# A MoE tail behind attention: two zero fills moved behind the last gather, a gate row broadcast through DRAM, and the last gate digits on POOL

## Chip, cores and metric

One core of a Trainium2 chip. The metric is device time in microseconds, the median of several executions. Engines are named as the profile names them: PE (TensorE), DVE (VectorE), ACT (ScalarE), POOL (GpSimd), SP (SyncE, which here only issues DMAs).

## The reference

Attention over 4 batches, 8 heads, 768 positions and head dimension 64, followed by a mixture of experts over the 3072 rows that come out.

```python
# attention: each query keeps 6 of 24 key chunks of 32, by an upper bound on its scores
ub = sum(max(q * k_min, q * k_max))            # one bound for each query and chunk
top_chunks = argsort(where(causal, ub, -1e9))[..., -6:]
attn = softmax(where(sel & causal, q @ k.T / 8, -1e9))
x = (attn @ v) laid out as (3072, 512)
# mixture of experts: 8 experts of 512 -> 1024 -> 512, top 1, capacity 80
expert_idx = argmax(x @ w_gate); gate_w = softmax(x @ w_gate)[expert_idx]
out = zeros((3072, 512))
for e in range(8):
    tok = rows of expert e; if more than 80: the 80 with the largest gate_w
    out[tok] = gate_w[tok] * (relu(x[tok] @ w1[e]) @ w2[e])
```

At most 640 of the 3072 output rows are computed; all others are zero. So the kernel writes zeros over the whole output (four fills of 1.5 MB, one for each batch of 768 rows) and then scatters the computed rows over them.

## The kernel before

**Order of the work.** Everything is written out by hand in one stream of `op(engine, ...)` calls. A helper, `Sync`, puts in the semaphore waits from the names that each operation reads (`r`) and writes (`w`). Each engine runs its own operations in the order in which they are written. DMAs are issued by SP (`"sp"`), by POOL (`"gpd"`), and at the start by ACT.

**The pair loop.** Sixteen pairs of heads (`i` from 0 to 15, four pairs for each batch) go through a software pipeline. For pair `i` PE computes the scores in six steps, of which ACT takes the exponentials (`scores`, L509, L524, L531); POOL masks the diagonal and adds up the denominators (`folds`, L545 and L554); PE multiplies by the values (`values`, L568), and ACT copies the product (L576). The bounds of the next pair (`bounds`, L472, and `bounds_out`, L479 to L491), the denominators and gate logits of the pair before (`sums`, L581 and L595, then L586 to L651 on DVE), and its rows (`rows`, L641 on PE, `scale_rows`, L661 on DVE and a DMA of SP to `x_rows` in DRAM) are woven in between. `take_q` (L439), `take_r` (L443) and `take_k` (L449 to L456) turn the loaded q and k for the pair after the next. SP loads q and k four pairs ahead and v two pairs ahead.

**Ranking by gate weight.** When a batch is complete, its tokens are ranked within each expert during the next batch's pairs. `kk` is the pair's place in its batch, `bb` the batch being ranked:

- `kk == 0`: the gate weights come out as `gt6`, one column for each of six tiles of 128 tokens (`gate`, L679 to L684). Then all 768 are needed as a row on every partition, `G[:, S:2S]`: `rank_row` does it with six PE transposes of a broadcast column (L716) and a copy by ACT (L718). `rank_own` (L726) is DVE's.
- `kk == 1`: `rank_pred` (L721, ACT) makes a second row, a hair smaller; `rank_cmp` (L741, DVE, six of them) and `rank_diag` (L734) compare each token with all others.
- `kk == 2`: `rank_count` (L791, PE) counts the winners for each expert; `rank_late` makes one-hot rows, digits of the gate weight in three bf16 parts (`gate_digits`, L687 to L690) and columns (`gate_cols`, L694, `gate_gcols`, L699).
- `kk == 3`: `table` and `merge` keep the best 80 of each expert.

**Loads and fills.** Expert weights are loaded with a cast to bf16 by POOL's DMA queue: `wload(e, 0)` is w1 of expert `e`, `wload(e, 1)` its w2, 1 MB each as written. The buffer of w1 of expert 6 holds zeros first, from which three fills are sent (after pairs 0, 1 and 12); the fourth fill comes from a part of `G`, zeroed by ACT at pair 14 (L955). The buffers of w1 of expert 7 and w2 of expert 6 hold the comparisons of `rank_cmp` and `rank_diag`. w2 of expert 7 comes in eight pieces (`last_w2`, L922), four at pair 15 and four among the experts.

**The tail.** The last batch has no later pairs to hide in. Its gate, `last_row` (L708 to L711), comparisons (`last_diag`, `last_low`, `last_high`, L753 to L768, on DVE and ACT), count (`last_count`, L775), table and merge follow the last pair, with `keep_warm` (L886), matmuls into an unused bank, between them. Then `gather` (L1091) fetches 80 rows for each of eight experts by indirect DMA of POOL, `turn` (L1100, L1104) transposes them, `up` (L1114, with ReLU at L1123 on ACT and L1125 on DVE) and `down` (L1138) are the two products. `down` runs in six rounds; DVE scales each round into one of four buffers `yv(r % 4)` (L1142), and POOL scatters it (L1144). Each scatter names all four fills in what it reads, so it waits until all zeros have landed. Gather `e` from 3 on waits for the copy of expert `e - 3`'s `turn`.

Of the kernel before, what the change touches and what calls it, by code (L numbers as in the profile page):

```python
# [147 lines left out]
def bass_quest_chunk_select__then__topk_capacity_drop_kernel(  # L148
# [57 lines left out]
    with ExitStack() as pers:  # L206
# [13 lines left out]

        sy = Sync(nc)
        op = sy.op

        with nc.Block() as blk:

            @blk.sync
            def _body(_unused):
# [41 lines left out]
                gt6 = al(pers, "gt6", [128, NT])  # L269
# [120 lines left out]
                op("dve", lambda: ve.memset(wg[:], 0.0), w=["wg"])  # L390
                op("dve", lambda: ve.memset(onc[:], 0.0), w=["onc"])
# [286 lines left out]
                def gate(b):  # L678
# [4 lines left out]
                    op("dve", lambda: ve.reciprocal(gt6[:], lsum[:]), r=["lsum"], w=["gt6"])  # L683
                    op("dve", lambda: ve.tensor_tensor(ohb[:, :, 0:E], oh[:], along(lmax), ALU.is_equal), r=["oh", "lmax"], w=["ohb"])  # L684

                def gate_digits(b):
                    op("dve", lambda: ve.tensor_copy(gsp[:, :, 0], gt6[:]), r=["gt6"], w=["gsp0"])  # L687
                    op("dve", lambda: ve.tensor_tensor(gdf[:], gt6[:], gsp[:, :, 0], ALU.subtract), r=["gt6", "gsp0"], w=["gdf"])
                    op("dve", lambda: ve.tensor_copy(gsp[:, :, 1], gdf[:]), r=["gdf"], w=["gsp1"])
                    op("dve", lambda: ve.tensor_tensor(gsp[:, :, 2], gdf[:], gsp[:, :, 1], ALU.subtract), r=["gdf", "gsp1"], w=["gsp2"])  # L690

                def gate_cols(b):
                    ohv = [bass.AP(ohb, 0, [[NT * 32, 128], [32, NT], [0, n], [1, E]]) for n in (2, 3)]
                    op("dve", lambda: ve.tensor_tensor(RC[:, :, 0:2, :], ohv[0], bass.AP(  # L694
                        idc, b * NT * 2, [[TOKT * 2, 128], [2, NT], [1, 2], [0, E]]), ALU.mult), r=["ohb", "idc0", "idc1"], w=["RCi"])

                def gate_gcols(b):
                    ohv = [bass.AP(ohb, 0, [[NT * 32, 128], [32, NT], [0, n], [1, E]]) for n in (2, 3)]
                    op("dve", lambda: ve.tensor_tensor(RC[:, :, 2:5, :], ohv[1], bass.AP(  # L699
                        gsp, 0, [[NT * 3, 128], [3, NT], [1, 3], [0, E]]), ALU.mult), r=["ohb", "gsp0", "gsp1", "gsp2"], w=["RCg"])  # L700
# [3 lines left out]
                def last_row():  # L704
                    for t in range(NT):
                        o = t * 128 if t < 3 else 128 + t * 128
                        gb = bass.AP(gt6, t, [[NT, 128], [0, 128]])
# [5 lines left out]
                def rank_row(b):  # L713
                    for t in range(NT):
                        gb = bass.AP(gt6, t, [[NT, 128], [0, 128]])
                        op("pe", lambda: pe.transpose(SC[1][:, ts(t)], gb, ident_f[:]),  # L716
                           r=["gt6", "ident_f"], w=["SC1"], inc=(t == NT - 1))
                    op("act", lambda: ac.activation(G[:, S:2 * S], SC[1][:, 0:S], ACTF.Copy), r=["SC1"], w=["grow"])  # L718
# [4 lines left out]
                def rank_own(b):  # L723
                    tq = bass.AP(triQ, 0, [[128, 128], [0, NT], [1, 128]])
                    gb = bass.AP(gt6, 0, [[NT, 128], [1, NT], [0, 128]])
# [189 lines left out]
                def fill(g, zs, zk):  # L915
                    zd = bass.AP(out.tensor, out.offset + g * NT * 128 * Dm, [[Dm, 128], [128 * Dm, NT], [1, Dm]])
                    op("sp", lambda: sp.dma_start(zd, zs), r=[zk], w=[f"outz{g}"], dsem=f"d_zero{g}")
# [12 lines left out]
                for i in range(NP):  # L930
# [10 lines left out]
                    if i == NP - 1:  # L941
                        wload(E - 1, 0)
# [5 lines left out]
                    if live and kk == 1:  # L948
                        rank_pred()
                        rank_cmp(bb, 5)  # L950
# [3 lines left out]
                    if i == NP - 2:  # L954
                        op("act", lambda: ac.activation(G[:, 0:Dm], bass.AP(ident_f, 0, [[128, 128], [0, Dm]]), ACTF.Copy, scale=0.0),  # L955
                           r=["ident_f"], w=["growP"])
# [9 lines left out]
                    if i:  # L966
# [3 lines left out]
                        scale_rows(i - 1)  # L970
                    if i == NP - 2:
# [176 lines left out]
                for e in range(3):  # L1148
                    gather(e)
# [59 lines left out]
```

## Time and profile before

| what | value |
|---|---|
| median of 3 runs | 290.12 us (290.0 to 290.32) |
| profiled execution: own time, span | 289.86 us, 288.1 us |
| instructions | 8696 |
| busy: PE, DVE, ACT, POOL | 274.3, 213.1, 147.0, 227.2 us |
| pair loop ends, last gather of x issued, last scatter issued | about 236, 270.85, 283.67 us |
| DMA in all | 47.95 MB, mean 166 GB/s |
| the transposes of L716 (18) and the copies of L718 (3) | 273 ns each, 811 ns each |

Times are counted from the start of the span. A timeline line has start, duration, engine, line, operation, tiles written and read, and the count of instructions merged into it; brackets give the idle time just before and what ended it. A line of a DMA issue list has the tiles, the queue, the count, the size, and the time from issue to landing. A line of windows has the stretch, its length, the busy time of PE, PEld (weight loads), DVE, ACT and POOL with their instructions, the granted clock, the share of the 16 DMA engines, and GB/s.

### The profile page before, as it was taken

What the parts mean: (1) busy time and instruction counts of PE and PEld (TensorE: products, weight loads), DVE (VectorE), ACT (ScalarE), POOL (GpSimd) and SP (SyncE); (2) the same over time, 40 slices, a digit from 0 to 9 for tenths busy, and PEclk for the clock granted to TensorE, in tenths of its full rate; (3) what the DMA queues carried; (4) which work ended last, traced back from release to release, by engine and by line L of the source; (5) the groups of instructions that cost most, each with busy time, mean ns of one, the idle gap of its engine ahead of it and who ended that gap; (6) DMA issues with size and microseconds to landing.
All of it is one profiled execution on the core that took longest, in us unless ns stands there. A gap on an engine that the chain in (4) does not pass through costs nothing.

```text
span 288.1 us, 8696 instructions
## 1 busy us (share of the span) xinstructions
PE 274.3 (95%) x3609; PEld 170.0 (59%) x3609; DVE 213.1 (74%) x575; ACT 147.0 (51%) x202; POOL 227.2 (79%) x295
## 2 busy tenths in 40 slices
PE   7899999999999999999999999999999999859991
PEld 7454656565656565656565656666656666428761
DVE  5897455566988989659889898898899888813341
ACT  2275656555576555555765555546756563403310
POOL 6079899998999999989999999899999970044732
PEclk9999999999999999999999999999999999998998
DMA  9999989999989999999999989995991599911361
GB/s 151 180 156 152 320 155 297 169 155 177 187 166 167 193 174 182 158 183 181 164 163 183 186 155 155 183 196 111 298 195 30 220 161 186 208 35 48 89 128 61
DMA packets 158359, 47.95 MB, mean 166 GB/s; under 512 B 142405, under 2 KB 150721, under 8 KB 158320
## 3 DMA queue, kind: packets, MB, share of 16 engines
q1 hardware_dynamic: 141664, 28.34, 50.9%
q0 software_dynamic: 13520, 18.67, 38.4%
q10 hardware_dynamic: 3136, 0.39, 0.9%
q8 instruction: 28, 0.46, 0.7%
q14 instruction: 11, 0.09, 0.1%
HBM read 53.49 MB, written 11.01 MB: 224 GB/s over the span
## 4 chain that ended last, share of the span: by engine, by line
PE 70%; POOL 15%; DVE 6%; DMA 4%; issue 2%; ACTq 1%; POOLq 0%; DVEq 0%
PE SC L509 22%; PE OB L568 19%; POOL ES L554 12%; PE SC L524 4%; PE M L595 4%; PE OB L1138 4%; PE SC L1114 4%; PE OB L641 3%; POOL EXB L545 3%; PE M L472 3%; DMA x_rows<-xp 2%; PE M L581 2%; PE MB L497 2%; DMA qn<-in_q_dram 1%; DMA qn<-x_rows,idx 1%
## 5 line engine op out<-in xcount | busy, mean ns | idle before, releaser
L531 ACT ACTIVATE EXB<-SC 128x1024 f32<-128x1024 f32 x96 | 86.2, 917 | 46.4 <-PE SC L524 45.1
L554 POOL TENSOR_TENSOR ES<-ES,EXB 128x256 f32<-128x256 f32 (+1 forms) x105 | 101.7, 980 | 4.8
L509 PE MATMUL SC<-qT,kT 64*128 64x512 f32 (+3 forms) x512 | 96.3, 466 | 0.1
L568 PE MATMUL OB<-EXB,vn 128*64 128x256 f32 (+3 forms) x704 | 72.8, 361 | 0.7 <-POOL EXB L545 0.7
L568 PEld LDWEIGHTS OB<-EXB,vn 128*64 128x64 f32 x704 | 46.9, 137 | 23.9 <-issue 9.8
L509 PEld LDWEIGHTS SC<-qT,kT 64*128 64x128 f32 x512 | 41.4, 186 | 23.0 <-issue 14.3
L554 POOL TENSOR_TENSOR ES<-EXB 128x768 f32<-128x768 f32 (+1 forms) x30 | 46.8, 1559 | 2.5
L524 PE MATMUL SC<-unsT,ind 64*128 64x128 bf16 (+5 forms) x256 | 37.7, 289 | 0.1
L576 ACT ACTIVATE oT<-OB 128x512 f32<-128x512 f32 (+1 forms) x32 | 15.6, 489 | 38.2 <-PE OB L568 38.2
L545 POOL TENSOR_SCALAR_AFFINE_SELECT EXB<-EXB 128x256 f32<-128x256 f32 x79 | 34.1, 442 | 0.0
L524 PEld LDWEIGHTS SC<-unsT,ind 64*128 64x128 bf16 x256 | 12.8, 95 | 17.9 <-issue 8.0
L439 DVE STREAM_TRANSPOSE qT<-qn 128x768 f32<-128x768 f32 x16 | 15.6, 974 | 7.2 <-PE SC L524 6.4
L586 DVE STREAM_TRANSPOSE M<-M 128x192 f32<-128x192 f32 x16 | 6.3, 394 | 19.2 <-PE M L595 18.9
L1091 POOL DMA_INDIRECT qn<-x_rows,idx x4 | 3.9, 987 | 20.8 <-DMA x_rows<-xp 19.0
L661 DVE TENSOR_TENSOR xp<-OB,rden 128x768 bf16<-128x768 f32 x16 | 15.3, 954 | 6.6 <-PE OB L641 6.3
L443 ACT ACTIVATE rq<-qT 128x768 f32<-128x768 f32 x16 | 13.5, 843 | 9.9 <-DVE qT L439 9.2
L449 DVE STREAM_TRANSPOSE kT<-kn 128x768 f32<-128x768 f32 x16 | 15.5, 966 | 1.2 <-DMA kn<-in_k_dram 1.2
L453 DVE TENSOR_REDUCE kmm<-kT 128x24 f32<-128x768 f32 x16 | 15.2, 950 | 0.5
L454 DVE TENSOR_REDUCE kmx<-kT 128x24 f32<-128x768 f32 x16 | 15.1, 942 | 0.0
L486 DVE MAX8 top<-M 128x8 f32<-128x8 f32 (+4 forms) x160 | 14.6, 164 | 0.6
L641 PE MATMUL OB<-ident_f,oT 128*128 128x128 f32 x96 | 13.9, 281 | 0.5 <-ACT oT L576 0.5
L456 POOL TENSOR_TENSOR kmm<-kmx,kmm 128x24 f32<-128x24 f32 x15 | 7.1, 471 | 9.2 <-DVE wg L907 9.2
(222 smaller groups left out, 415.6 us busy)
## 6 DMA issues: line engine op xcount, KB each, us to landing
w1s<-in_moe_w_dram POOLq DMA_DIRECT2D x8, 1024.0 KB, 9.8
w2s<-in_moe_w_dram POOLq DMA_DIRECT2D x7, 1024.0 KB, 11.2
vn<-in_v_dram SPq DMA_DIRECT2D x32, 192.0 KB, 4.8
kn<-in_k_dram SPq DMA_DIRECT2D x62, 96.0 KB, 2.7
qn<-in_q_dram SPq DMA_DIRECT2D x62, 96.0 KB, 3.1
out_dram<-w1s SPq DMA_DIRECT2D x3, 1536.0 KB, 7.8
x_rows<-xp SPq DMA_DIRECT2D x16, 192.0 KB, 6.1
out_dram<-G SPq DMA_DIRECT2D x1, 1536.0 KB, 6.9
```

The lines of the kernel that those rows point to most:

```text
L439: op("dve", lambda: ve.transpose(qT[j][:], qn[s][:].rearrange("p a b c -> p (a b c)")), r=[f"qn{s}{g}" for g in range(4)], w=[f"qT{j}"])
L449: op("dve", lambda: ve.transpose(kT[j][:], kn[s][:].rearrange("p a b c -> p (a b c)")), r=[f"kn{s}{g}" for g in range(4)], w=[f"kT{j}"])
L453: op("dve", lambda: ve.tensor_reduce(kmm[j][:, 0, 0:NCH], kv, AX, ALU.min), r=[f"kT{j}"], w=[f"kmm{j}"])
L509: op("pe", lambda: pe.matmul(o, kT[j][pr, ts(kt)], qT[j][pr, q0:q1], start=True, stop=False), r=[f"kT{j}", f"qT{j}"], w=[f"SC{s}"], inc=False)
L524: op("pe", lambda: pe.matmul(o, ind[pr, ts(kt)], unsT[j][pr, b0 - 128:q1 - 128], start=False, stop=True), r=[f"ind{h}", f"unsT{j}"], w=[f" ...
L531: op("act", lambda: ac.activation(Ex(st, None, 0, W), src, ACTF.Exp, scale=SCALE), r=[f"SC{s}"], w=[f"E{st}"])
L545: op("gp", lambda: gp.affine_select(ad, a, pattern=[[0, 2], [1, 128]], compare_op=ALU.is_ge, fill=0.0, base=0, channel_multiplier=-1), r=[ ...
L554: op("gp", lambda: gp.tensor_tensor(o, in0, in1, ALU.add), r=[f"E{s2}", f"E{first[0]}"] if first else [f"E{s2}"] + kt, w=kt)
L568: op("pe", lambda: pe.matmul(OB[pr, q0:q1], vn[s][:, kt, h, :], ex, start=(n == 0), stop=last), r=[f"vn{s}{h}", "ES0" if st is None else f ...
L576: op("act", lambda: ac.activation(oT[:, q0:q1], OB[:, q0:q1], ACTF.Copy), r=[f"O{bk}"], w=[f"oT{bk}"])
L641: op("pe", lambda: pe.transpose(OB[:, ts(t)], oT[:, ts(t)], ident_f[:]), r=["oT0", "oT1", "ident_f"], w=[f"O{t // 4}"], inc=(t in (3, NT - ...
L661: op("dve", lambda: ve.tensor_tensor(xo, xi, rx, ALU.mult), r=["O0", "O1", "rden"], w=[f"xp{i % 2}"])
```

## The change

Four things change together.

1. *Gate row, batches 0 to 2.* `rank_row` goes. `gt6` gets 32 columns (zeroed at the start). `row_out` transposes it on DVE in blocks of 32 and sends it to DRAM in token order; `row_in` reads 768 values back to all 128 partitions. Both DMAs are issued by SP. `rank_pred` and the first `rank_cmp` move to later places in `kk == 1`.
2. *Fills.* The fills of batches 2 and 3 leave pairs 12 and 14. ACT zeroes a part of `ES` behind the first three gathers, and SP issues both fills after the last gather has landed. The scatters of rounds 0 and 1 are issued by POOL after that point.
3. *Loads.* w1 of expert 6 is loaded at pair 13 in place of 14, w1 of expert 7 at the end of pair 14 in place of pair 15.
4. *Tail of the last batch.* The digits and columns go to POOL; `gate_gcols` comes earlier; the first product of `values` for the last block comes after `last_row`; `last_low(3)` comes first of ACT's; and the count takes tile 4 last, with four warming matmuls ahead of it in place of six behind.

```diff
+        gd = nc.dram_tensor("gate_row", [32 * 128], F32, kind="Internal").ap()
-                gt6 = al(pers, "gt6", [128, NT])
+                gt6 = al(pers, "gt6", [128, 32])
+                gtT = al(pers, "gtT", [128, 32])
+                op("dve", lambda: ve.memset(gt6[:], 0.0), w=["gt6"])
...
+                def on(b):
+                    return ("gp", gp) if b == B - 1 else ("dve", ve)
+
                 def gate_digits(b):
-                    op("dve", lambda: ve.tensor_copy(gsp[:, :, 0], gt6[:]), r=["gt6"], w=["gsp0"])
+                    e, q = on(b)
+                    op(e, lambda: q.tensor_copy(gsp[:, :, 0], gt6[:, 0:NT]), r=["gt6"], w=["gsp0"])
...
-                def rank_row(b):
-                    for t in range(NT):
-                        gb = bass.AP(gt6, t, [[NT, 128], [0, 128]])
-                        op("pe", lambda: pe.transpose(SC[1][:, ts(t)], gb, ident_f[:]),
-                           r=["gt6", "ident_f"], w=["SC1"], inc=(t == NT - 1))
-                    op("act", lambda: ac.activation(G[:, S:2 * S], SC[1][:, 0:S], ACTF.Copy), r=["SC1"], w=["grow"])
+                def row_out():
+                    op("dve", lambda: ve.transpose(gtT[:], gt6[:]), r=["gt6"], w=["gtT"])
+                    o = bass.AP(gd.tensor, gd.offset, [[32, 4], [128, 32], [1, 32]])
+                    op("sp", lambda: sp.dma_start(o, gtT[:]), r=["gtT"], w=["gd"], dsem="d_gd")
+
+                def row_in():
+                    a = bass.AP(gd.tensor, gd.offset, [[0, 128], [1, S]])
+                    op("sp", lambda: sp.dma_start(G[:, S:2 * S], a), r=["gd"], w=["grow"], dsem="d_gr")
...
-                    if i == NP - 1:
-                        wload(E - 1, 0)
                     folds(i, 0, 1)
...
-                    if live and kk == 1:
-                        rank_pred()
-                        rank_cmp(bb, 5)
                     scores(i, 2, 4)
...
-                    if i == NP - 2:
-                        op("act", lambda: ac.activation(G[:, 0:Dm], bass.AP(ident_f, 0, [[128, 128], [0, Dm]]), ACTF.Copy, scale=0.0),
-                           r=["ident_f"], w=["growP"])
...
                         scale_rows(i - 1)
+                    if live and kk == 1:
+                        rank_cmp(bb, 5)
                     if i == NP - 2:
-                        fill(3, bass.AP(G, 0, [[2 * S, 128], [0, NT], [1, Dm]]), "growP")
                         rank_late(bb)
                     if live and kk == 0:
                         gate_exp()
                         gate(bb)
+                        row_out()
...
+                    if live and kk == 0:
+                        row_in()
                     if i + 4 < NP:
                         load(i + 4, "qk")
...
                     if live and kk == 1:
+                        rank_pred()
                         rank_diag(bb)
...
-                    if live and kk == 0:
-                        rank_row(bb)
-                    if 0 < i < NP - 3:
+                    if 0 < i < NP - 2:
                         wload((i - 1) // 2, (i - 1) % 2)
                     if i == NP - 2:
-                        wload(E - 2, 0)
                         wload(E - 2, 1)
-                    if i in (0, 1, 12):
+                        wload(E - 1, 0)
+                    if i in (0, 1):
...
-                values(NP - 1, (1,), (0, 1), False)
                 gate(b)
                 gate_cols(b)
+                gate_digits(b)
                 sort_take()
-                gate_digits(b)
+                gate_gcols(b)
                 last_row()
-                values(NP - 1, (1,), (1, 9), False)
+                values(NP - 1, (1,), (0, 9), False)
                 last_high(0)
+                last_low(3, "act")
                 last_low(5, "act")
                 values_out(1)
                 last_low(4, "act")
-                last_low(3, "act")
...
                 scale_rows(NP - 1)
-                gate_gcols(b)
-                last_count((0, 5, 1, 4, 2, 3), (0, 0, 0, 0, 0, 6))
+                last_count((0, 5, 1, 3, 2, 4), (0, 0, 0, 0, 4, 0))
...
+                    if r > 1:
+                        scatter(r)
+
+                def scatter(r):
                     op("gpd", lambda: gp.indirect_dma_start(
...
                 for e in range(3):
                     gather(e)
+                op("act", lambda: ac.activation(bass.AP(ES, 0, [[2 * S, 128], [1, Dm]]), bass.AP(ident_f, 0, [[128, 128], [0, Dm]]), ACTF.Copy, scale=0.0),
+                   r=["ident_f"], w=["zero", "D0", "U0", "D1", "L1", "U1"])
...
                             if e + 4 == E - 1:
+                                for g in (2, 3):
+                                    fill(g, bass.AP(ES, 0, [[2 * S, 128], [0, NT], [1, Dm]]), "zero", xgk(E - 1))
                                 last_w2(range(4, FB))
+                                for r in range(2):
+                                    scatter(r)
```

## The prediction

> **What bounds the kernel now.** I read the page's engine line first, then the chain of waits, and then the timelines of POOL, DVE, SP and PE around the places that the change touches.
>
> ```profile
> PE 274.3 (95%) x3609; PEld 170.0 (59%) x3609; DVE 213.1 (74%) x575; ACT 147.0 (51%) x202; POOL 227.2 (79%) x295
> ```
>
> TensorE is busy nearly throughout, but that is no proof that it alone sets the pace. POOL's timeline at the turn of pairs 4 and 5:
>
> ```profile
> 84.03 0.95 POOL L456 TENSOR_TENSOR kmm<-kmx,kmm 128x24 f32<-128x24 f32 x1
> 84.93 0.91 POOL L420 DMA_DIRECT2D w2s<-in_moe_w_dram  x1
> 86.26 0.40 POOL L545 TENSOR_SCALAR_AFFINE_SELECT ES<-EXB 128x256 f32<-128x256 f32 x1 [0.43 <-PE M L595]
> ```
>
> The bracket is all the slack that POOL has in this pair; until 100.6 it has no other gap. An ordinary pair takes 13.9 us on PE, with 0.4 to 0.6 us idle on POOL. DVE in pair 5, where the gate row is used:
>
> ```profile
> 87.23 2.04 DVE L741 TENSOR_SCALAR w2s<-G,gt 128x640 bf16<-128x640 f32 x1
> 89.29 0.96 DVE L661 TENSOR_TENSOR xp<-OB,rden 128x768 bf16<-128x768 f32 x1
> ...
> 90.90 0.98 DVE L439 STREAM_TRANSPOSE qT<-qn 128x768 f32<-128x768 f32 x1 [0.65 <-PE SC L524]
> ```
>
> From 90.90 DVE has no gap until the comparisons end at 102.1, and PE starts the count (L791) at 102.55. So over this batch it is PE's scores, then DVE's 11.2 us, then PE's count that set the pace. The first comparison costs nothing today: the rows for L661 come from PE at 89.26.
>
> The tail is different. The chain of waits has:
>
> ```profile
> 248.64 5.52 DMA x_rows<-xp
> 254.22 0.61 issue
> 255.05 2.75 DMA qn<-x_rows,idx
> 258.17 0.83 PE SC L886 x2
> ```
>
> The last attention rows take 5.52 us to land; the gathers wait on them. The windows show a DMA share over 1 from 233 to 252: three expert loads of 1 MB and four pieces of 128 KB run then. Writing the same rows at 220.9, with the DMA engines idle, took 2.9 us. PE stands still from 254.7 to 257.85 and then runs at half clock:
>
> ```profile
> 259.00:260.00 1.00, 1.00 (x19) 1.00 (x17) 0.00 (x0) 0.00 (x0) 0.57 (x1) 0.50 0.32 82
> ```
>
> (The last three columns are granted clock, DMA share and GB/s.) At the end, POOL scatters each round as soon as DVE has written it:
>
> ```profile
> 269.53 1.02 POOL L1144 DMA_INDIRECT out_dram<-EXB,idR  x1 [0.92 <-ACT kT L1123]
> 270.85 0.98 POOL L1091 DMA_INDIRECT kn<-x_rows,idx  x1 [0.30 <-issue]
> ...
> 283.67 0.97 POOL L1144 DMA_INDIRECT out_dram<-EXB,idR  x1 [2.16 <-DVE EXB L1142]
> ```
>
> **What the Trainium skill says.** "SBUF — State Buffer", section "SBUF: two separate sides": the port pair shared by DVE and GpSimd is an exclusive lock held for the whole instruction, and the loser blocks. The trace agrees: the 2.04 us of L741 above end 0.35 us after a POOL addition (87.11 to 88.92) has ended, while its five sisters take 0.55 to 0.91. "DMA: Bandwidth & Descriptors", section "Issuing engines are not separate DMA queues": all queues run on the same 16 engines and interleave; the 5.52 us against 2.9 agree. "TensorE: Matmul & The Clock Gate", section "What's actually happening": an idle window of about 3.4 us halves the clock; here 3.1 us of idleness were followed by about 3.4 us at 0.5.
>
> **Gate row, three batches.** Removed for each: six transposes, 0.66 us of PE (82.08 in the chain), and ACT's copy, 0.81 us. ACT has gaps in these pairs, so the copy itself gives nothing; I found PE later by 0.66 over L568 to L595, no more. Added: a 32-column DVE transpose, about 0.17 us by the reciprocal's 0.19; DVE idles 1.27 us before the next L586, but L726 ends that much later, and POOL's L456 (0.95 instead of 0.24 beside it) with it. So POOL's 0.43 gap leaves about 0.25 of the 0.66. In pair 12 POOL has no marked gap: about 0. The memset of gt6 lies in DVE's wait for the first load (before 4.65).
>
> Then DVE: the first comparison moves behind L661. With PE 0.66 earlier L661 ends at 89.6; the comparison meets a POOL addition (89.4 to 90.6) and ends near 91.0, against a take_q start of 90.90 before. DVE's chain, and so the count on PE, is then no earlier. rank_pred moves into ACT's gap after L443 (1.2 us) and costs nothing unless that gap goes; then oT is later.
>
> SP: row_out and row_in are two issues of some 0.55 us, and SP stands between them until the row has landed, about 3 us by x_rows' 2.9 to 3.2. Behind it stand the q and k loads for four pairs on; they are used two pairs later (28 us), so this is covered. At batch 0 SP reaches row_out only at 82.0 (x_rows ends its issue there), so row_in goes out near 85.1, beside the expert load of 84.93, and 393 KB land near 89.5 by an estimate of 4.5 us (v pieces of 192 KB took 3.2 to 5.4). DVE wants them at 89.6. Batches 1 and 2 have 4 us or more in hand. **Body: 0**, bounds −1.3 (three times POOL's 0.43) and +2 (DVE waiting for the row).
>
> **Loads and tail.** w1 of expert 6 goes out in pair 13, 14 us earlier, and one of the three issues leaves the end of pair 14 and pair 15 (0.8 us on POOL, beside PE's longer work). One MB at some 200 GB/s is 5.2 us less DMA work before 252, so the last x_rows finds idle engines: issued near 248.4, landed near 251.3. That isn't all gained. The four digit operations (0.7 us) and two column products (0.5 us) leave DVE; on POOL, idle from 236 to 255, they cost some 2 us (six at L456's 0.24 and as much again between them is 2.9 at most) and are done by 245.5, needed at 250. But the count now has 4 warming matmuls of 0.21 us ahead of its last group, and PE gets there later since ACT has one more pair of operations (1.1 us) before oT. My walk along PE gives a count finished at 249.65, against DVE's L796 at 248.75: idx at 252.5 instead of 251.5. The gather goes out 0.8 later, 253.3 instead of 255.05: **−1.75**. PE then waits 0.5 us, not 3.1, so the half-clock stretch (up to 1.2 us; the third gather's landing limits it) gives **−0.85**. The experts run 2.6 us earlier.
>
> **Fills and scatters.** Two fills leave the middle of the kernel, where nothing on the chain waited for them: 0. They return behind gather 7. That gather needs turn(4), whose copy ends at 268.63, now 266.0; with 0.8 to wake and 2.6 to land, 269.4. One fill alone:
>
> ```profile
> out_dram<-G SPq DMA_DIRECT2D x1, 1536.0 KB, 6.9
> ```
>
> and one microsecond of the windows while it ran:
>
> ```profile
> 226.00:227.00 1.00, 1.00 (x17) 0.61 (x12) 0.52 (x3) 0.04 (x1) 1.00 (x3) 1.00 1.04 381
> ```
>
> About 1.2 us pass before it moves data, and then the engines are full at 380 GB/s. So two are not hidden in each other: 3.15 MB / 380 GB/s = 8.3 us, after 270.6. The four pieces of w2 (issued by POOL from 267.8) take about 2 us of this (0.5 MB at 200 GB/s, part of it before 270.6), and 0.2 for the end: **both zeroes landed at 281.1**. Every scatter waits for all zeroes. POOL stands with scatter 0 from about 270, and the other five are queued behind it. Round 4's product writes the buffer of round 0, so DVE waits for scatter 0 to land, the ReLU of expert 7 is queued behind it, and PE's last product behind that. From 281.1: 0.85 for POOL to start (as 254.2 to 255.05), 2.9 to land, 0.75 and 0.5 on DVE, 48 matmuls 1.35 at full or 2.7 at half clock after this long wait, taken as 2.0, 0.6 for the last copy, 0.8 to the scatter: last scatter at 289.5 against 283.67. The serial scatters on POOL, six at 1.3 us, come out 0.4 earlier, so DVE's way decides. With the 4.4 us from there to the end (283.67 to 288.1) the span is 294.0, **+5.9 us**: own time 289.86 + 5.9 = 295.8. The median shown lies 0.26 above the profiled execution's own time: **296.0**.
>
> **Rivals.** (a) *Faster:* the fills land before they hold anything. From the landing to the last scatter I have 8.4 us, so the point is a landing at 275.3, 5.8 before mine. If two fills took the 6.9 us of one, with w2 beside them, it would be 276.3; with the body at −2.0 (PE's transposes in full) and idx not delayed (−0.9) 273.4, so an end at 286.2 and 288.2 us as median. For it: PE's 95%, and the fact that packets of different queues interleave. Against it: the share of 1.04 while one fill ran alone. (b) *The row comes late:* each us by which row_in misses 89.6 stops DVE and with it the count; 1 us in each batch on top gives 299. For it: SP's loads in this stretch took up to 9.6 us. Against it: batches 1 and 2 are early. (c) *A smaller loss:* w2 costs the fills nothing, the clock stays up and the body gives 1.3: 292.5. The transposes' 0.66 us not arriving at all is part of the forecast, not a rival.
>
> **Numbers.** Forecast with (c) 0.75, (b) 0.10, (a) 0.12, and 0.03 for an end within 0.2% (0.6 us, about what a measurement of this kernel can tell from no change). The range runs from 291.5 (below (c)) to 299.0.
>
> **What would show it.** Right: x_rows' last landing near 3 us; PE without half clock at 258; L741's first comparison behind L661 and L791 no earlier in its batch; out_dram from ES landing some 11 us after gather 7; POOL idle about 10 us before scatter 0; DVE idle before the fifth L1142; PE idle some 8 us ahead of the last product. Wrong: the fills landed before round 3 is written, or pairs 5, 9 and 13 shorter by 0.5 us or more, or longer by 1.

## The result, and the profile after

| | before | after |
|---|---|---|
| median of runs | 290.06 us (289.51 to 290.32) | 299.69 us (297.57 to 303.46) |
| profiled execution: own time, span | 289.86, 288.1 us | 298.05, 296.3 us |
| pair loop ends (denominators of the last pair, PE) | 236.65 | 235.92 |
| gather 0, gather 7 issued | 255.05, 270.85 | 252.76, 266.05 |
| last scatter issued | 283.67 | 291.81 |

The ratio is 1.031, interval 1.0221 to 1.04: slower, as forecast, and by more than forecast. Ratios here leave out runs more than 1.5% above the fastest of the same kernel, in after the one of 303.46 us, whose mean granted clock (0.971) is no lower than that of the others (0.966 to 0.975). The other three are 297.57, 298.05 and 301.33; the median of all four is 299.69, that of the three 298.05. That the three lie almost 4 us apart, where before stays within 0.8, is part of what has to be explained.

In after, lines moved a little: the comparisons are L753, `scale_rows` L665, `row_out` and `row_in` L726 and L730, gathers L1097, ReLU of DVE L1131, `down` and its scaling L1144 and L1148, scatters L1154, fills L929. The page's engine line:

```profile
PE 272.6 (92%) x3589; PEld 168.0 (57%) x3589; DVE 210.1 (71%) x573; ACT 144.8 (49%) x199; POOL 228.4 (77%) x301
```

PE has 1.7 us less to do and the kernel is 8 us longer: nothing here is decided by busy time. **The pair loop**, the timelines of POOL and DVE where they were shown of before:

```profile
85.12 0.91 POOL L424 DMA_DIRECT2D w2s<-in_moe_w_dram  x1
86.05 0.41 POOL L549 TENSOR_SCALAR_AFFINE_SELECT ES<-EXB 128x256 f32<-128x256 f32 x1
```

```profile
88.81 0.96 DVE L665 TENSOR_TENSOR xp<-OB,rden 128x768 bf16<-128x768 f32 x1 [1.90 <-PE OB L645]
89.69 1.07 DVE L753 TENSOR_SCALAR w2s<-G,gt 128x640 bf16<-128x640 f32 x1
90.68 0.96 DVE L443 STREAM_TRANSPOSE qT<-qn 128x768 f32<-128x768 f32 x1
```

POOL's bracket is gone: it was the 0.43 us of slack. POOL now sets the pace of the pair, and over the whole chain of waits its additions make 22% of the span where they made 12%. The first comparison stands behind L665, and DVE's next step starts 0.22 us earlier than before (90.68 against 90.90). SP in the same pair:

```profile
70.87 8.16 SPq L368 DMA_DIRECT2D kn<-in_k_dram  x4
...
81.40 0.65 SPq L726 DMA_DIRECT2D gate_row<-gtT  x1
84.21 0.35 SPq L730 DMA_DIRECT2D G<-gate_row  x1
```

The transposed gate column was ready at 78.1, but SP was issuing four loads of k for 8.2 us, then v and `x_rows`, and sent it at 81.40; then SP stood until it had landed and asked for it back at 84.21. The row landed 3.7 us later, 1.8 us ahead of DVE. In the next two batches the margins were 2.8 us (issued 140.60, 3.4 to land, wanted at 146.76) and 2.0 us (198.76, 3.9, 204.71). In this execution the row is in time; it is close.

**The tail.** The windows, with the columns as before:

```profile
259.00:260.00 1.00, 1.00 (x25) 0.68 (x25) 0.49 (x1) 0.34 (x1) 0.69 (x2) 1.00 0.11 27
270.00:271.00 1.00, 1.00 (x26) 0.72 (x26) 0.48 (x1) 0.38 (x1) 0.00 (x0) 1.00 1.19 150
275.00:276.00 1.00, 1.00 (x26) 0.58 (x19) 0.00 (x0) 0.00 (x0) 0.00 (x0) 1.00 1.07 408
280.00:281.00 1.00, 0.00 (x0) 0.00 (x0) 0.00 (x0) 0.00 (x0) 0.00 (x0) 0.50 0.25 90
281.00:282.00 1.00, 0.00 (x0) 0.00 (x0) 0.00 (x0) 0.00 (x0) 0.00 (x0) 0.50 0.07 27
```

At 259 the clock is 1.00 where it was 0.50. SP issues the fills from 269.49 on, but at 270 the DMA engines are full at only 150 GB/s: the four pieces of w2, which POOL issued from 267.01 to 269.27, are in front (e4, below, shows the same fills without them). At 275 the fills have the engines full at 408 GB/s. From 280 on the engines are nearly empty, at a share of 0.25 and then 0.07, and yet the zeros have not landed. The chain of waits:

```profile
266.05 3.42 DMA kn<-x_rows,idx
...
269.91 12.81 DMA out_dram<-ES
...
283.63 2.74 DMA out_dram<-EXB,idR
...
286.46 0.75 DVE EXB L1148
...
287.66 1.04 PE OB L1144 x8
288.71 1.73 PE SC L1144 x19
...
290.53 0.50 DVE EXB L1148
```

Gather 7, then a fill that lands 12.81 us after its issue, then scatter 0, DVE, the last product and the last copy. POOL's timeline has the same from its side:

```profile
266.05 0.96 POOL L1097 DMA_INDIRECT kn<-x_rows,idx  x1 [2.30 <-ACT kT L1129]
...
283.63 1.04 POOL L1154 DMA_INDIRECT out_dram<-EXB,idR  x1 [14.37 <-DMA out_dram<-ES]
...
291.81 0.98 POOL L1154 DMA_INDIRECT out_dram<-EXB,idR  x1 [1.97 <-DVE EXB L1148]
```

POOL stands for 14.37 us in front of scatter 0; before, that scatter went out at 266.29.

### The profile page after: what moved, and what is told of

It reads as the page before. It is cut to its first block, busy times and chain, and to the rows that moved or that the text cites. A ratio compares the mean times of both kernels' runs of the same rounds, so it can differ in the third digit from the quotient of the medians.

```text
span 296.3 us, 8665 instructions
## 1 busy us (share of the span) xinstructions
PE 272.6 (92%) x3589; PEld 168.0 (57%) x3589; DVE 210.1 (71%) x573; ACT 144.8 (49%) x199; POOL 228.4 (77%) x301
## 4 chain that ended last, share of the span: by engine, by line
PE 50%; POOL 29%; DMA 9%; DVE 5%; issue 3%; ACT 1%; ACTq 1%; POOLq 0%; SPq 0%; DVEq 0%
POOL ES L558 22%; PE SC L513 16%; PE OB L572 14%; POOL EXB L549 5%; DMA out_dram<-ES 4%; PE SC L528 3%; PE M L599 3%; PE OB L645 3%; PE M L476 2%; PE OB L1144 2%; DMA qn<-in_q_dram 1%; PE M L585 1%; DMA kn<-x_rows,idx 1%; PE MB L501 1%; POOL kmm L460 1%
## 5 line engine op out<-in xcount | busy, mean ns | idle before, releaser
L572 PEld LDWEIGHTS OB<-EXB,vn 128*64 128x64 f32 x704 | 46.8, 137 | 24.3 <-issue 10.2
L665 DVE TENSOR_TENSOR xp<-OB,rden 128x768 bf16<-128x768 f32 x16 | 15.3, 955 | 12.3 <-PE OB L645 12.3
L1154 POOL DMA_INDIRECT out_dram<-EXB,idR x6 | 6.0, 996 | 17.6 <-DMA out_dram<-ES 14.4
L1148 DVE TENSOR_SCALAR EXB<-OB,gR 128x512 f32<-128x512 f32 (+1 forms) x6 | 4.2, 706 | 18.8 <-DMA out_dram<-EXB,idR 12.2
```

The source lines that it names most:

```text
L572: op("pe", lambda: pe.matmul(OB[pr, q0:q1], vn[s][:, kt, h, :], ex, start=(n == 0), stop=last), r=[f"vn{s}{h}", "ES0" if st is None else f ...
L665: op("dve", lambda: ve.tensor_tensor(xo, xi, rx, ALU.mult), r=["O0", "O1", "rden"], w=[f"xp{i % 2}"])
```

## The experiments

Each was timed beside before on the same chip and at the same time. The median of before lay between 289.8 and 292.1 us on these occasions, so the ratio to before is what is compared. "Transposes back" means `rank_row` in the place of `row_out` and `row_in`.

| run | ratio to before | interval | runs in it |
|---|---|---|---|
| after | 1.031 | 1.0221 to 1.04 | 3 of 4 |
| e1: late fills of a sixth of the rows | 1.0036 | 1.0003 to 1.007 | 5 of 10 |
| e2: after, fills early | 1.023 | 1.0193 to 1.0267 | 6 of 6 |
| e3: after, six output buffers | 1.0284 | 1.024 to 1.0328 | 6 of 6 |
| e4: after, pieces of w2 behind gather 5 | 1.0578 | 1.0547 to 1.0609 | 6 of 6 |
| e5: before + gate row by SP | 1.0155 | 1.0115 to 1.0196 | 6 of 6 |
| e6: after, transposes back | 1.0297 | 1.0268 to 1.0325 | 4 of 6 |
| e7: e6, fills early | 0.9917 | 0.9889 to 0.9946 | 3 of 6 |
| e8: before + early loads | 0.9895 | 0.9856 to 0.9934 | 7 of 8 |
| e9: e6, one fill late | 1.0145 | 1.0119 to 1.0171 | 6 of 6 |
| e10: e6, PE kept warm | 1.029 | 1.0266 to 1.0313 | 5 of 5 |
| e11, e13: before + gate row by ACT | 1.0487, 0.9967 | 1.045 to 1.0523, 0.995 to 0.9984 | 6 of 6, 16 of 18 |
| e12: e8 + digits by POOL | 0.9889 | 0.9865 to 0.9913 | 4 of 6 |
| e14: before + gate row by ACT and SP | 0.997 | 0.9949 to 0.9991 | 13 of 14 |
| e15: after, gate row by ACT | 1.0267 | 1.0235 to 1.0299 | 6 of 6 |
| e16: e8 + gate row by ACT | 1.0053 | 1.0028 to 1.0079 | 8 of 8 |

**e1, fewer zeros late.**

```diff
-  zd = bass.AP(out.tensor, ..., [[Dm, 128], [128 * Dm, NT], [1, Dm]])
+  zd = bass.AP(out.tensor, ..., [[Dm, 128], [1, Dm]])     # both late fills
```

> The changed kernel, but each of the two late fills writes only the first 128 of its 768 rows (the other rows of these two batches are left without zeros). Theory: the landing of the late fills sets the end, and everything else in the change is a gain; then the fills land about 4 us after gather 7, before the scatters would have been issued anyway, and the last scatter goes out where PE's last product allows, 3.35 us earlier than in the kernel before (last up at 275.52 against 278.87): about 280.3, span near 284.7, time near 286.5 (ratio 0.987), and the spread between runs falls back to under 1 us. Rival: a part of the loss comes from the gate row, the loads or the order of the tail; then the time stays above 290.

It came to 1.0036 (the five runs in it have a median of 291.5 us; all ten lie between 288.3 and 300.4), not to the 286.5 of the theory. So most of the loss does hang on the bytes of the late fills, but some 5 us stay without them. The profiled execution (294.21 us) shows two reasons. The first is in its chain:

```profile
272.57 6.76 DMA out_dram<-ES
```

Even a sixth of the bytes lands 6.76 us after its issue, 7.2 after gather 7 and not 4, and POOL still stands 7.78 us in front of scatter 0. The pieces of w2 are in front here too: from 272 to 275 the engines are full, or nearly, at 124 to 173 GB/s. The second is the gate row, for which DVE waited 3.1 us once.

**e2, fills early again.**

```diff
-  if i in (0, 1):
+  if i in (0, 1, 10, 12):     # fills 2 and 3 from the zeros in w1 of expert 6
-  for g in (2, 3): fill(g, ...ES...)     # behind gather 7
```

> The changed kernel with its two late fills sent from the middle again, after pairs 10 and 12 out of the zeros in w1 of expert 6, whose load stays at pair 13; scatters 0 and 1 directly behind their rounds. Theory: as with the small fills, 286.5 us. Rival 1: the fills in the middle cost the pair loop something that the move had saved; then over 287.5. Rival 2: the load of w1 of expert 6 now waits for the second of these fills, and POOL with it; then pair 14 is 1 us or more longer.

1.023, 296.9 us: a miss by 10 us. With no late fill, the kernel is still almost 7 us slower than before. SP's queue and DVE's waits in its profile:

```profile
184.68 12.08 SPq L368 DMA_DIRECT2D qn<-in_q_dram  x4
...
201.06 0.52 SPq L726 DMA_DIRECT2D gate_row<-gtT  x1
208.53 0.34 SPq L730 DMA_DIRECT2D G<-gate_row  x1
```

```profile
DVE w2s L753 <- DMA G<-gate_row: 7.5, 1, 7.5
```

Behind the first of the two fills, four loads of q held SP for 12.08 us (2.55 in after), and the write of the third batch's row went out 5 us later than in after (196.04). Then the write, 16 KB, took some 7 us to get out to DRAM, SP stood for it, and DVE stood 7.5 us for the row. The rival's wait, POOL's for a fill that still read the zeros, was there too but small (1.7 us).

**e5, the gate row alone.** Before, with `row_out` and `row_in` in place of `rank_row` and the two moves of the first comparison and of `rank_pred` that belong to them, and nothing else of the change. (The cut leaves out the moves.)

```diff
-  if live and kk == 0: rank_row(bb)
+  row_out()     # behind gate(bb), both DMAs by SP
+  row_in()      # ahead of load(i + 4, "qk")
```

> The kernel before with the gate row through DRAM alone (and the two moves of the first comparison and of the smaller row that belong to it). In the profile of the changed kernel the pair loop ended 0.7 us earlier, but in the four experiments so far DVE's first comparison waited 3.1 to 7.5 us for the row in one or two batches, which that profile does not show. Theory: the row's two transfers stand in SP's queue behind loads[...], the row comes late in some executions and not in others, and each late row stops DVE and the pair loop. Then this kernel runs between 289 us (no late row) and 297, with a spread of 3 us or more against under 2 of the kernel before, median near 292. Rival: the late rows come from the fills and loads having been moved about them; then the row alone gives 289 us with the spread of before.

1.0155, 294.1 us, runs 3 us apart: the row by SP costs over 4 us by itself. The profile, DVE's timeline and then the comparisons of the next microseconds taken as one line:

```profile
91.57 0.85 DVE L747 TENSOR_SCALAR w2s<-G,gt 128x640 bf16<-128x640 f32 x1 [1.84 <-DMA G<-gate_row]
...
99.66 5.50 DVE L747 TENSOR_SCALAR w1s<-G,gt 128x640 bf16<-128x640 f32 x5
```

```profile
L747 DVE TENSOR_SCALAR w1s<-G,gt x5: 573/792/1981, 99.7 to 103.7; 128x640 bf16<-128x640 f32 x5
```

DVE waits 1.84 us, and of this only 0.86 is left when the other five comparisons start (99.66; 98.80 before). But now they take 5.50 us in place of 3.30: least, median and longest are 573, 792 and 1981 ns, against 554, 572 and 903 before. POOL's additions of the next pair start at 100.80 and 103.43 and last 1.93 and 1.38 us; the late comparisons lie beside both, where the punctual ones ran mostly between two additions (one until 99.4, the next from 101.84). It fits what the Trainium skill says in "SBUF — State Buffer", section "SBUF: two separate sides", on the port pair of DVE and GpSimd, whose loser waits out the other's instruction; that it is this port was not tried apart. DVE ended 3.1 us late (105.08 against 102.02), and PE's count behind it. The price of a late row is therefore not one for one: 1.84 us became 3.1.

**e6 and e7, all but the row.** The transposes back in after (e6), and the fills early as well (e7, behind pairs 9 and 11).

```diff
-  row_out(); row_in()
+  rank_row(bb); rank_pred() and rank_cmp(bb, 5) where before has them
```

> The changed kernel with the six transposes and ACT's copy back in place of the row through DRAM; late fills, early loads and the new tail stay. Theory: the late fills cost what they cost in the profile of the changed kernel, less nothing: the loop ends 0.7 to 0.9 us later than there, the rest is the same: 299 us, and the spread between runs goes to 1.5 us or less. Rival: the spread of the changed kernel comes from the landing of the fills; then it stays at 3 us or more.

> As the last, and the two late fills sent from the middle again (behind pairs 9 and 11, out of the zeros in w1 of expert 6, which is still loaded at pair 13), the scatters directly behind their rounds: of the change there stay the early loads and the new order of the tail with POOL's digits. Theory: x_rows lands before the last table is merged, gather 0 goes out 1.5 to 2.3 us earlier than in the kernel before, PE keeps its clock, and the scatters follow PE: 286.5 to 287 us, spread under 1.5 us. Rival: fills behind pairs 9 and 11 hold back q, k and v; then 289 or more.

e6: 1.0297, and the four runs in it lie from 298.50 to 299.84, 1.3 us apart. Without the row the loss stays, so it is the fills'; the spread is smaller, but that it is the row's alone is not shown (e15). e7: 0.9917. Between the two, the late fills alone are worth 0.038 of 290 us, **11 us**. With the row by SP the same step is worth only 0.008, some 2 us (after against e2), because in e2 the row then comes late: the two losses do not add up. (The early fills of e2 stand one pair later than those of e7; what that is worth was not tried apart.)

**e9, the price of one fill.**

```diff
-  if i in (0, 1):          fill(i, ...)
+  if i in (0, 1, 12):      fill(min(i, 2), ...)
-  for g in (2, 3):
+  for g in (3,):
```

> The kernel after with the transposes back, and one of the two late fills sent early again (after pair 12, from the zeros in the buffer of w1 of expert 6); the other still goes out behind the last gather. Theory (scatter 0 waits for the last zero, and the bytes set when it lands): one fill lands some 8 us after its issue (1.2 to start, 4.1 for 1.5 MB, 2 for the pieces of w2, 1 for a slow end) in place of 13, so that everything behind it comes 4 to 5 us earlier: 294.5 us against 299.0 with both late. Rival: the slow end of the fills and POOL's standing cost the same for one as for two: 298 or more. Second rival: with one fill the tail is no longer bound by it, and the time falls to the 288 of no late fill.

1.0145, where before has 290.1 that is 294.3: as expected. The chain of e9, and of e6 for the pair of fills:

```profile
271.28 8.62 DMA out_dram<-ES
```

```profile
270.77 12.96 DMA out_dram<-ES
```

The second fill costs 4.3 us, which for 1.57 MB is 366 GB/s. If the first one's bytes take as long (an estimate), the other 4.3 of its 8.62 us are a price that one late fill pays as well as two: the start, the pieces of w2 and the end.

**e3, more buffers.** A buffer for each round, so that no round waits for an earlier scatter.

```diff
-  EXB, 2048 + (r % 4) * 512     w=[f"y{r % 4}"]
+  EXB, 2048 + r * 512           w=[f"y{r}"]
```

> The changed kernel with six output buffers in place of four, so that round 4 needs no buffer that scatter 0 still reads. Theory: behind the landing of the fills (282.7 in the changed kernel) two chains run side by side, DVE's (scatter 0 lands, round 4, ReLU, PE's last product at half clock, round 5) and POOL's (six scatters, 1.3 us apart). Taking the first away leaves the second: last scatter 7.4 us behind the landing, 290.1 in place of 291.8, time 1.7 us less than the changed kernel. Rival: only the wait of DVE matters and POOL's queue is not dense; then more than 4 us less. Rival: the fills alone, with nothing behind them, make the loss; then no difference.

The first and the last of POOL's scatters:

```profile
286.08 1.04 POOL L1154 DMA_INDIRECT out_dram<-EXB,idR  x1 [13.84 <-DMA out_dram<-ES]
...
292.60 0.98 POOL L1154 DMA_INDIRECT out_dram<-EXB,idR  x1 [0.30 <-issue]
```

6.52 us from first to last, 1.3 for each, against 8.18 in after, and the last goes out 7.4 us behind the landing, as expected: the way through DVE and PE is worth 1.7 us, and right behind it POOL's own issuing decides. The total (1.0284) can't be told from that of after, whose interval it shares; this profile also has a row 3.7 us late.

**e10, the clock of the last product.**

```diff
+  if last and fb == 4 and c0 == 0:
+      keep_warm(44, MBf[:, 0:512], "MB")     # in the middle of the last product
```

> The kernel after with the transposes back, and with 44 warming matmuls into an unused bank (9.4 us) put in the middle of the last product, where PE stands still for 10 us. Theory: the last product's second half ran at half clock, 2.8 us where 1.4 would do at full; with the clock up the end comes 1.2 us earlier: 297.8 us against 299.0. Rival: DVE's and POOL's part of the chain behind the first scatter (six scatters 1.3 us apart) decides instead, and the time moves by less than 0.4.

The clock stayed at 1.00 until the end, and nothing came of it: 1.029. In the chain the last product takes 3.4 us (289.07 to 292.50) against 2.8 in e6, and 1.65 of it is put down to a single last matmul, although in PE's timeline the last matmuls end at 291.12. What held DVE's release until then is open. So the half clock is seen in after, but that it costs anything is not shown.

**e4, the pieces of w2 moved.**

```diff
+  if e + 4 == 5: last_w2(range(4, FB))     # behind gather 5, not behind the fills
```

> The changed kernel with the last four pieces of w2 of expert 7 issued behind gather 5, some 5 us ahead of the fills, in place of behind gather 7. Theory: they took about 2 us of the DMA engines beside the fills (150 GB/s at a share over 1 from 269 to 272), so both fills land about 2 us earlier and the kernel ends 2 us earlier. Rival: the last fill is held up by something else at its end (the DMA share is 0.25, 0.07 and 0.02 in the last three microseconds before it lands); then it gains under 0.7 us.

1.0578, much slower, by a fault of the edit: `last_w2` names `kT0` among what it reads, ACT's ReLU in expert 2 writes it, and so ACT waited for the pieces (4.53 us until 274.88) and gather 7 for ACT. It says one thing on the side: with no pieces beside it, the last fill took 10.77 us in place of 12.81, so the pieces are worth about the 2 us that the prediction gave them. The windows of e4 show both ends of the fills, issued at 283.05 and 283.47:

```profile
284.00:285.00 1.00, 1.00 (x31) 0.84 (x31) 0.37 (x2) 0.59 (x2) 0.00 (x0) 1.00 1.00 379
...
292.00:293.00 1.00, 0.00 (x0) 0.00 (x0) 0.00 (x0) 0.00 (x0) 0.00 (x0) 1.00 0.38 129
293.00:294.00 1.00, 0.00 (x0) 0.00 (x0) 0.00 (x0) 0.00 (x0) 0.00 (x0) 1.00 0.05 20
```

They are at 379 GB/s within a microsecond, where after had 150. But the slow end is there too: the landing comes at 294.24, some 2 us after the engines stop being full. So it is not the pieces of w2 that make it; what does stays open.

**e8 and e12, early loads alone.** Before with w1 of experts 6 and 7 a pair earlier and the fills behind pairs 9 and 11; in e12, digits and columns on POOL as well.

```diff
-  if i == NP - 1: wload(E - 1, 0)
-  if 0 < i < NP - 3:
+  if 0 < i < NP - 2:
-      wload(E - 2, 0)
       wload(E - 2, 1)
+      wload(E - 1, 0)
-  if i in (0, 1, 12):
+  if i in (0, 1, 9, 11):
```

> The kernel before with the early loads alone (w1 of expert 6 at pair 13, of expert 7 at the end of pair 14), which needs the fills behind pairs 9 and 11; its own tail. Theory: x_rows no longer shares the DMA engines, so gather 0 is set by the table of DVE, idx at 251.5: out at 252.4 in place of 255.05; with PE's clock up 3.5 us less than before, 286.3 us, or 0.3 to 0.8 less than with the new tail, whose count comes 0.9 us later for its four warming matmuls. Rival: the new tail is worth its 0.7 us of digits on DVE; then this is slower than the last by 0.5 us or more.

> The kernel before with the earlier weight loads, the two fills early, and of the new tail only the digits and columns on POOL (with the gate columns ahead of the row), no warming matmuls ahead of the last group of the count. Theory: DVE loses 1.2 us of work ahead of the count, gather 0 goes out up to 1 us earlier than at 252.8, and the time is 286.0 us against 286.7. Rival: DVE wasn't what the count waited for, and nothing is gained: 286.7.

e8, at 0.9895 (286.7 us), is faster than both kernels. Its chain has the gathers waiting for the indices and no longer for `x_rows`:

```profile
252.61 0.17 DVE idR L1076
252.81 0.35 POOL qn L1085
```

e12 adds nothing that can be told (0.9889): DVE did lose the work, but gather 0 goes out at 252.74 all the same. The new tail of e7 is no better than the old one of e8 either; in e7 gather 0 leaves at 253.66, with four warming matmuls and a group of the count ahead of DVE's ranks.

**e11, e13, e14: who issues the row.** All are e5 with other queues.

```diff
-  op("sp", lambda: sp.dma_start(o, gtT[:]), ...)
+  op("acd", lambda: ac.dma_start(o, gtT[:]), ...)             # e11, e13, e14
-  op("sp", lambda: sp.dma_start(G[:, S:2 * S], a), ...)
+  op("acd", lambda: ac.dma_start(G[:, S:2 * S], a), ...)      # e11, e13
```

> The kernel before with the gate row through DRAM alone, as in the run with the row only, but both its transfers issued by ACT instead of SP, so that they stand behind no load of k. Theory (the row is late because SP's queue is full when its turn comes): the row lands well before DVE's first comparison in all three batches, and the time is that of before, 290.3 us (289.7 to 291.0), with runs within 1 us of each other, against 294.1 by SP. Rival: the row's transfers themselves are slow beside the loads on the same 16 engines, whoever issues them: 293 to 295 again.

> The kernel before with the gate row through DRAM alone, DVE's transposition where the change has it (behind the gate), and both transfers issued by ACT, the first behind its rq copy of the pair and the second behind the turn of the chunk masks. In the earlier run by ACT the transposition had moved with the transfers behind DVE's key bounds, and ACT stood 4.7 us for it; that is mended here. Theory 1 (SP's queue makes the row late): the row is sent at 79.9, read from 83.1, and lands in time; 290.5 us on a chip where before has 290.1, runs within 1 us. Theory 2 (the 16 engines' backlog makes it late, whoever issues it; the read landed 6.9 to 9.7 us after its issue in the earlier run by ACT): the read lands at 91 or later where DVE wants it at 89.7, and the time is 292 to 295.

> As the run before it, but the read of the row stays with SP, in its place ahead of the q and k loads; only the write goes by ACT. Theory 1: the write no longer stands behind v and x_rows in SP's queue, SP does not stand for it, and the row lands near 86.5, in time in every batch: 290.0 to 291.0 us. Theory 2: the write is as late by ACT as it was by SP (its landing took 2.8 to 7.5 us), and the row is still late in some batches of some runs: 292 to 294, with runs 2 us or more apart.

e11 (1.0487) is slow by its own edit: DVE's transposition had moved with the transfers behind DVE's key bounds, ACT stood 4.7 us for it, and PE stood for ACT. With that mended, e13 comes to 0.9967 and e14 to 0.997, the runs in the ratio 2.0 and 1.5 us apart (those of before beside them 2.9). The row by ACT is not merely harmless, it gains 1 us on before. ACT's queue in e13:

```profile
79.07 1.08 ACTq L719 DMA_DIRECT2D gate_row<-gtT  x1
...
82.33 0.35 ACTq L723 DMA_DIRECT2D G<-gate_row  x1
```

The row is sent at 79.07 and asked for at 82.33, where e5 by SP has 83.08 and 85.87. Its landing is no quicker (4.2 to 4.6 us in the three batches): it is the same bytes on the same engines. DVE waits for it nowhere. As e14 moves only the write and gains as much, it is SP's queue ahead of the write that makes the row of e5 late. The transfers themselves are a second part: the read took up to 6.9 us in e1 and 7.1 in e3 where after has 3.4 to 3.9, and by ACT 8.2 to 9.7 in e11 and up to 7.9 in e16. A row sent early has room for this. The Trainium skill, in "DMA: Bandwidth & Descriptors", section "Issuing engines are not separate DMA queues", says that another issuing engine saves only the sequencer's time, usually little. The runs agree on the landing, but here that time is 4 us, because the sequencer was occupied with loads of k.

**e15 and e16, the row by ACT in after, and in e8.** The same edit as e13.

> The kernel after, whole, with only both transfers of the gate row given to ACT in place of SP. Theory: what SP's queue cost the changed kernel goes, and the rest stays: a ratio to before of 1.026 (299.0 of the run with the transposes back, less 0.9 for PE's transposes), that is 297.5 to 298.5 where before has 290.1, with runs within 1.5 us of each other in place of 4 to 6. Rival: the spread and the last few us come from the late fills and stay: 299 to 300, runs 3 us or more apart.

> The kernel before with the earlier weight loads, all four fills early (after pairs 0, 1, 9 and 11), the old tail, and the gate row through DRAM with both transfers by ACT. Theory: the gains add up, 0.9895 from the loads and 0.997 from the row: 0.9865, that is 286.2 where before has 290.1. Rival: w1 loaded a pair earlier makes the row late for batch 2 again, and nothing is gained over the loads alone: 287 or more.

e15: 1.0267, runs 2.9 us apart (296.7 to 299.6; those of before 2.1). The median fits the theory, the spread does not quite, and the interval overlaps that of after: that the row costs after its last us or two is likely, not shown. e16 missed: 1.0053, slower than e8. Its chain has another loss:

```profile
193.11 3.52 DMA vn<-in_v_dram
...
200.93 12.70 DMA vn<-in_v_dram
```

PE waits for v. SP spent 11.96 us from 173.31 on four loads of q behind the fill of pair 9 (from 168.45 and 9.68 in e8), issued the first of these v 8.8 us later than e8 (193.11, 184.34), and the next v and fill 2.7 us later. DVE waited 0.5 us for a row once, so the rival's wait was there but is not the loss. Why the same fills push SP further back here stays open. The gains of loads and row did not add up.

## Why the prediction failed

The direction and the mechanism were right: the late zeros hold every scatter, and that costs more than the tail gains. What failed is sizes: the landing of the zeros, put 1.6 us too early for want of their slow end; the last product, 0.8 us too short; and the distance of the median from the profiled execution, put at 0.26 us and measured at 1.64. The forecast of 296.0 was 3.7 us short of the median of 299.69. The first two are read from the profile; what makes the third is not shown. In the order of the steps:

- **Body, 0: too timid.** In after the loop ends 0.73 us earlier, three times the quarter of a microsecond that POOL's slack left; the prediction had found it and then let DVE cancel it. e13, with the loop 0.7 us shorter, has the row nowhere late and gains 1 us.
- **Gather 0 at 253.3, gather 7 landed at 269.4:** measured 252.76 and 269.47. `x_rows`' last landing fell from 5.5 to 3.5 us and PE kept its clock, as forecast. That the second number fits is luck: the experts ran 0.7 earlier, and gather 7 took 3.42 to land, not 2.6. e7 and e8 bear the step out: without row and late fills the kernel gains 0.8 to 1%, where 2.6 us was forecast.
- **Fills landed at 281.1: the step that failed.** Measured 282.72. The term was bytes by rate, with 2 us for w2 and 0.2 for the end. The rate was right (379 to 415 GB/s from 273 to 279) and the 2 us too (e4), but the end takes 2.7 us, from 280, when the share falls to 0.25, to 282.72; the bulk was done some 0.9 us sooner than forecast, or the miss would be larger. The 0.2 had no reading behind it. The fill that the prediction shows took 6.9 us; its own 1.2 to start and 4.1 for the bytes (1.57 MB at 380 GB/s) leave 1.6 us of it, which the sum does not have. Of the miss inside the profiled execution (span 296.3 against 294.0) this step is 1.6 us.
- **From the landing to the last scatter, 8.4 us: measured 9.1.** The 48 matmuls took 2.8, not 2.0; the forecast had taken a value between full and half clock, and the clock was 0.50. (That the clock is the reason is not shown: in e10 it was 1.00, and the product took no less.) The other pieces agree: 0.9 to start, 2.74 to land, 0.75, 0.50. That is 0.7 us, and with the 1.6 it makes the 2.3 that the profiled execution lies above the 295.8 of the forecast.
- **The median beside the profiled execution, +0.26: mis-sized.** Own time 298.05 against a median of 299.69. The forecast took over the small spread of before. With four runs, one at 301.33 and one at 303.46, the 1.64 us is also chance: the median of the three runs in the ratio is the 298.05 of the profiled one. The runs of after, e2, e3 and e5, all with SP's row, lie 3.0 to 3.8 us apart, those of e6, without it, 1.3.
- **Rival (b), the row late, given 0.10,** came true in other executions than the profiled one, and is a likely part of that spread. Its defence was wrong: "batches 1 and 2 have 4 us or more in hand", but in the profile of after these margins are 2.8 and 2.0 us, and in e2 and e3 the row of batch 2 is late by 7.5 and 3.7. For batch 0 the prediction had read SP's queue rightly (row out at 82.0, measured 81.40). Nor is the price one us for one: in e5 1.84 became 3.1. But the row does not carry the miss: without it (e6) or with it by ACT (e15) the ratio is still 1.0297 and 1.0267, 298.7 and 297.8 us where before has 290.06.
- **The idle times** that were to show it are there and longer than forecast, by what the fills were late: POOL 14.4 us ahead of scatter 0 (10 forecast), PE 10.2 ahead of the last product (8), DVE 12.2 ahead of the fifth round's scaling.
- **Rivals (a) and (c)** fall: the zeros landed 7.4 us after the point from which (a) would have decided; w2 cost the fills its 2 us, and the clock did go down.

What stays open: what makes the end of the fills slow, how much of the spread of after is the row (e15 still has 2.9 us, against 2.1 of before beside it), and what held the end of e10's last product.

## What to carry to other kernels

Before a transfer is given to a queue, read what that queue has ahead of it and how long each issue takes there: here an engine that issues bulk loads held a small transfer behind them for 4 us, and a write with a read that depends on it stands in that queue twice. All scatters wait for the landing of the last zero, so zeros that were free in the middle of this kernel cost 11 us at its end, and the last of them came 2.7 us after the engines stopped being full: a sum of bytes by rate needs a term for the end. Where something arrives late, look also at what the delayed work now lies beside: 1.84 us became 3.1 because five comparisons slid onto POOL's additions.

## What the hardware showed that had not been expected

- The end of two fills of 1.5 MB is slow: after some 7 us at 379 to 415 GB/s the DMA share falls to 0.25, 0.07 and 0.02, and the landing comes 2.7 us later (some 2 us in e4, with no other load beside it). One fill landed 8.62 us after its issue (e9), two 12.8 to 13.0, and two of a sixth of the bytes still 6.76 (e1).
- Four loads of 128 KB issued 0.8 to 2.5 us ahead of the fills kept the DMA engines full, or nearly (shares of 1.13, 1.19 and 0.79), at 142 to 174 GB/s for the 3 us from 269 to 272, where the fills alone move 379 (e4, from 284 on).
- A transfer of 16 KB took some 2.8 us to DRAM in one batch (after) and some 7 us in another (e2), and SP stood for it.
- Comparisons that otherwise took 572 ns took up to 1981 ns beside POOL's additions (e5).
